# Memory attention and a bilinear feed-forward on one core: heads of batches 2 to 7 grouped by row half, three transposes for the means of k and v, and a new work list

## The chip, the cores and the metric

The kernel runs on one core of a Trainium2 chip. The metric is device time in microseconds (us) from the start of an execution to its end; the time given is the median of three executions. Beside it stands one execution that the hardware profiler recorded.

The engines are named as the profile names them: PE (matrix products), PEld (its weight loads), DVE (vector), ACT (scalar, activation functions), POOL (GpSimd) and SP (which issues transfers here). Each takes its instructions in the order in which the program lists them.

## The reference

For 8 batches, 8 heads, 576 tokens, head dimension 64 and 32 memory slots, all in float32:

```python
a = exp(phi - max(phi)); a = a / (sum(a, slots) + 1e-9)
k_m = einsum('bhsm,bhsd->bhmd', a, k)      # 32 weighted sums of k per head
v_m = einsum('bhsm,bhsd->bhmd', a, v)
scores = (q @ k_m.T) / sqrt(64)
attn = softmax(scores, slots)
x = (attn @ v_m), heads joined: 4608 tokens x 512
out = ((x @ w_a) * (x @ w_b)) @ w_out      # 512 -> 1536 -> 512
```

## The kernel before

**Per batch.** A batch has its heads on chip as 4 columns hp with two heads each: r = 0 on rows 0 to 63, r = 1 on rows 64 to 127. The eight heads are split into two groups g of four (j = 0 to 3). Inside a group every head has 32 rows (its memory slots) of the 128. Which head stands at (g, j) is told by `head(g, j)`; before, it crosses the two row halves: the heads of one group lie alternately on rows 0 to 63 and 64 to 127.

1. `exp_phi` (list name `exp`): exp of phi on ACT.
2. Means of k and v. In batches 2 to 7, `kv_sums` (`kv`, L286): 72 products on 64x32 tiles of PE into two banks `pkv`, one for each group; `take_kv` (`km`, L313, L318) divides on DVE and writes `rep`, six blocks of 128 columns: the even and odd columns of the k means for each group, each repeated four times, and the v means for each group, repeated twice; `kv_transpose` (`kvt`, L326, L327) turns the six blocks on PE with the identity into a bank `pT` and copies them to `kvT` on DVE. In batches 0 and 1, whose inputs come in halves, `sums` and `transpose` (`ks`, `vs`, `kt`, `vt`, L340 to L361) do the same in smaller parts.
3. `q_transpose` (`qt`, L269) turns q on DVE; `scores` (`sc`, `s`, L375) multiplies it with kvT on 32x32 tiles; `exp_scores` (`e`) takes exp on ACT. The division by the sum over slots has two forms: `denominators` and `normalise` (`den`, `nr`), or in batches 4 to 7 `ed`, `sm`, `tn`, `ad`. The result is the tile `A` of the batch.
4. `fold` (`v`, `hv`, L447) multiplies the means of v straight into w_a and w_b on 64x32 tiles, into banks `pva`; `take_fold` (`x`, `hx`, L460) copies them to `vab` on ACT and DVE.

**Feed-forward.** `up_half` (`a` and `b` with batch, block of 128 inner columns, half of the tokens; L621): two full products of 288 columns for each of `pa` and `pb`; ACT copies `pa` (L625), DVE multiplies with `pb` into `ht` (L628). The down projection works on pairs of blocks of 128 tokens in a seven-product scheme (`two_downs`, `d`, L550), 42 products of 256 columns for a pair. It takes sums of `ht` (`sum_tokens`, L534), which run on DVE where the list says `g` and on POOL where it says `h`, and sums of w_out (`T`, `V`).

**Order.** Nothing reorders the work: the string `PLAN` is walked from left to right (L632), and each word issues its instructions to the queues of their engines. A word such as `3kvt` is unit `kvt` of batch 3, `a2.5.1` is `up_half`, `d4` takes four products of the down projection, `F5` issues five idle products of 512 columns and `f5` five of 128 columns on a tile of zeros (`fill`, L211). Words such as `p1`, `k1`, `q1.0`, `v1`, `w256:512`, `o1` issue loads on POOL; `M` is a memset on POOL (L639).

Accumulators live in eight PSUM banks that are handed out in turn; tiles in `mid` have two buffers.

Of the kernel before, what the change touches and what calls it, by code (L numbers as in the profile page):

```python
# [25 lines left out]
f3 F1 O 0exp0 f1 f1 F2 p1 f2 f6 F7 w0:256 f2 f1 k1 f1 F3 0exp1 F5 f2 0qt0 q1.0 0ks0 0ks1 F5 0kt0 0qt1 M F2 0s0  # L26
w256:512 0qt2 0kt1 0e0 0den00 0qt3 0s1 0e1 F4 0den01 1exp0 0vs0 q1.1 0vt0 v1 0vs1 1exp1 F6 0nr00 0den10 0vt1
0den11 0hv0a 0hx0a 0nr10 0hv0b 0hx0b 0nr11 a0.1.0 b0.1.0 a0.0.0 F4 0nr01 1ks0 1ks1 b0.0.0 0hv1a 0hx1a 1kt0 1kt1
1qt0 1qt1 a0.0.1 a0.2.1 F1 b0.0.1 1s0 a0.1.1 0hv1b 1qt2 1qt3 0hx1b 1s1 1e0 1e1 b0.2.1 1den0 a0.2.0 b0.1.1 b0.2.0
1den1 1vs1 1vs0 1vt1 1nr0 1vt0 1nr1 a0.3.1 a0.3.0 1hv1b 1hx1b 1hv0b 1hv0a 1hx0a w512:1024 1hx0b b0.3.1 b0.3.0  # L30
1hv1a 0v1a 1hx1a 0x1a a1.0.0 a1.1.1 a1.1.0 a1.0.1 b1.0.0 b1.1.1 b1.1.0 a1.3.0 b1.0.1 a1.3.1 b1.3.0 b1.3.1 a0.5.0
0v1b 1v1a w1024:1536 0x1b 1x1a a1.2.0 1v1b 0v2a 1x1b o1 0x2a a0.7.1 b0.5.0 b1.2.0 b0.7.1 a0.7.0 b0.7.0 o5 a1.5.0
a1.2.1 b1.2.1 b1.5.0 a0.4.0 a0.6.0 b0.4.0 a0.4.1 a1.4.0 b0.6.0 b1.4.0 a0.9.1 0v2b 1v2b 1v2a 0x2b 1x2b a1.5.1
b0.4.1 1x2a b0.9.1 a0.8.0 a1.4.1 b1.5.1 o2 a0.5.1 a0.6.1 b0.8.0 a0.9.0 b0.6.1 b0.9.0 b1.4.1 a1.7.1 b0.5.1 b1.7.1
a0.8.1 b0.8.1 o0 a1.7.0 a0.10.0 b1.7.0 b0.10.0 a0.11.0 a1.9.0 o3 o4 b0.11.0 g0.0 b1.9.0 a1.6.1 k2 a1.6.0 p2 h0.3
a0.11.1 b1.6.1 b0.11.1 a1.8.1 a0.10.1 b1.6.0 v2 b1.8.1 g0.1 T01 a1.8.0 T00 V20 q2 T21 d1 2exp0 a1.9.1 d3 b0.10.1
p3 a1.10.0 d2 V10 g0.2 V11 d1 b1.9.1 2exp1 d1 a1.11.1 k3 d1 q3 T31 T30 d1 b1.10.0 b1.8.0 d1 b1.11.1 d4 h1.0 d2
2kv d4 2km d3 a1.11.0 d10 a1.10.1 2qt0 3exp0 d1 2kvt d2 h1.1 d1 2qt1 d12 2qt2 d3 2qt3 b1.10.1 g1.2 b1.11.0 v3 d1
2sc 2e0 d1 g1.3 d3 g2.0 d3 2e1 d1 2den0 h2.1 d8 p4 d8 2nr0 2den1 g2.2 2v0 2x0a 2x0b d2 2nr1 d10 2v1 d5 2x1a 3qt0
d3 g2.3 d3 2x1b d1 a2.3.0 a2.2.0 b2.3.0 b2.2.0 q4 k4 v4 a2.5.0 3exp1 b2.5.0 d2 3qt1 d4 a2.0.0 b2.0.0 d3 h3.0  # L40
a2.1.0 a2.4.0 2v2 3kv 3qt3 2x2a 3qt2 b2.1.0 2x2b d2 a2.11.1 a2.6.0 d4 3km a2.8.0 d1 q5 b2.4.0 d3 b2.6.0 d2 4exp0
d5 b2.11.1 d5 h3.1 d2 b2.8.0 a2.11.0 3kvt d2 a2.8.1 a2.7.1 b2.8.1 d2 a2.9.0 b2.7.1 3sc 3e1 3e0 g3.3 d1 b2.11.0
4qt0 a2.7.0 d2 a2.5.1 b2.5.1 b2.7.0 h3.2 3den0 d1 3nr0 4qt3 d1 b2.9.0 d2 a2.0.1 4qt2 a2.10.0 b2.0.1 p5 a2.4.1
b2.10.0 d1 k5 a2.10.1 d3 b2.10.1 d3 h4.0 4exp1 d1 a2.2.1 b2.4.1 3den1 d4 3v1 3x1a 4kv 3v0b 3x1b d3 3x0b d1 3nr1
d6 4km0 h4.1 a2.6.1 b2.2.1 a2.9.1 4qt1 a2.1.1 3v0a 3v2 d1 3x0a d2 3x2a d2 b2.6.1 3x2b d4 a3.9.0 d4 a3.5.0 d2
4km1 h4.2 b2.9.1 d1 a2.3.1 4kvt d1 b2.1.1 d1 b2.3.1 d2 5qt0 4sc a3.11.0 d1 h4.3 b3.5.0 5qt2 d5 4e1 d1 4e0 d1 v5
d6 b3.9.0 a3.0.0 g5.0 d1 h5.1 d3 4ed b3.11.0 d1 a3.3.0 d2 a3.10.1 b3.0.0 h5.2 5exp0 4sm0 q6 a3.1.0 d1 b3.3.0 d4
a3.3.1 d2 p6 d2 b3.10.1 a3.8.1 h5.3 d1 b3.3.1 b3.1.0 a3.6.0 b3.6.0 a3.7.0 a3.10.0 b3.8.1 d1 a3.1.1 b3.7.0 5qt1
d2 a3.8.0 a3.2.0 b3.10.0 d3 5exp1 a3.4.0 d1 b3.8.0 b3.1.1 d2 b3.2.0 k6 b3.4.0 4v0a 5kv 4x0a d1 a3.2.1 5km0
a3.4.1 5km1 d3 h6.0 h6.1 b3.2.1 d1 a3.9.1 d3 a3.5.1 d1 b3.4.1 b3.9.1 d5 4v0b 4x0b 4tn0 4v1 d1 h6.3 d3 4x1a d1  # L50
4x1b d2 a3.11.1 5kvt d1 p7 4sm1 a3.7.1 h6.2 d1 v6 d3 a3.6.1 d2 b3.5.1 b3.11.1 d1 5qt3 4v2 d4 4tn1 a3.0.1 d7 4x2a
4ad 6exp0 d1 b3.0.1 d6 4x2b b3.7.1 a4.11.0 b3.6.1 d1 a4.9.0 6exp1 d1 6qt0 b4.11.0 a4.7.0 a4.4.0 d4 b4.9.0 k7 d1
5sc 5e1 d1 5e0 d1 a4.0.0 d1 b4.4.0 d1 b4.0.0 a4.2.0 b4.2.0 d1 b4.7.0 d3 6qt1 d2 a4.4.1 d2 q7 a4.1.1 b4.4.1 5v0
5x0a 5x0b 6kv 5v1 h7.0 5x1a d3 6km0 a4.10.1 d1 5ed 6km1 d2 h7.3 h7.1 b4.1.1 h7.2 g8.0 d1 5x1b d2 h8.1 d1 a4.6.1
d4 b4.6.1 d4 a4.8.0 a4.5.0 5sm0 d1 v7 d1 h8.2 b4.10.1 a4.8.1 b4.8.0 a4.3.1 b4.5.0 d2 6qt3 d7 5v2 d2 5x2a d2
a4.1.0 d2 b4.3.1 7qt0 a4.3.0 d1 5x2b d1 b4.8.1 d1 7qt2 d1 b4.3.0 a4.5.1 d2 a4.10.0 b4.1.0 d2 6kvt 7exp0 d2 5tn0
d3 5sm1 a4.0.1 b4.5.1 d1 6qt2 d2 b4.0.1 d1 a4.6.0 d3 a4.7.1 d5 h8.3 d1 b4.10.0 d1 7exp1 d2 5tn1 d1 7qt1 a4.11.1
d3 6sc d5 6e1 d5 a4.2.1 d1 b4.7.1 d1 b4.6.0 5ad d1 a4.9.1 d1 h9.0 d1 b4.2.1 d3 6e0 b4.11.1 d1 b4.9.1 d1 a5.2.0
d1 a5.2.1 6ed g9.1 d1 b5.2.0 6v0a 6x0a 6v0b 7kv 6x0b b5.2.1 a5.11.0 b5.11.0 a5.8.0 a5.9.0 b5.8.0 h9.2 d1 7km0 d1
a5.3.0 d1 h9.3 d2 b5.9.0 b5.3.0 d2 a5.6.0 d1 g10.0 d1 h10.1 b5.6.0 a5.3.1 h10.3 d4 b5.3.1 d2 a5.1.0 d5 7qt3 d4  # L60
a5.7.0 d1 7km1 a5.7.1 b5.7.1 d9 b5.7.0 a5.5.0 d3 b5.1.0 d4 6sm0 b5.5.0 d3 a5.0.0 a5.1.1 d1 a5.10.0 d1 b5.0.0
7kvt d3 a5.0.1 d2 h10.2 b5.1.1 b5.0.1 d6 b5.10.0 a5.11.1 a5.10.1 6sm1 a5.4.0 d2 6v1 b5.10.1 6x1a d3 b5.4.0 d2
6x1b d1 b5.11.1 d1 a5.5.1 a5.9.1 6v2 6x2b b5.5.1 d1 6tn1 d1 a5.8.1 d1 6tn0 a5.6.1 d1 6x2a a5.4.1 d1 6ad b5.9.1
d4 7sc d1 7e1 7e0 b5.6.1 d2 b5.4.1 b5.8.1 a6.7.0 d1 7ed a6.9.0 7v0a 7v1 g11.0 d2 7x1a d2 g11.1 d2 a6.10.0 h11.3
h11.2 d1 h12.0 d3 7x0a 7sm0 a6.0.0 d2 b6.7.0 d2 b6.10.0 d4 b6.9.0 d5 a6.3.0 d7 a6.11.0 b6.11.0 b6.0.0 d1 a6.2.0
d5 b6.2.0 d1 a6.8.0 d1 b6.3.0 d1 7x1b d1 a6.5.0 h12.1 a6.10.1 b6.5.0 d4 7sm1 d4 h12.2 d3 a6.6.1 d2 g12.3 d3
b6.8.0 d6 a6.4.1 d3 b6.4.1 a6.9.1 d2 7tn1 b6.10.1 d1 7tn0 d3 7ad d2 b6.6.1 a6.2.1 a6.3.1 d1 a6.1.0 d1 b6.3.1
b6.2.1 d2 b6.9.1 d5 a6.8.1 a6.4.0 b6.1.0 b6.8.1 a6.11.1 b6.4.0 a6.6.0 b6.6.0 h13.0 a6.1.1 h13.1 a6.5.1 b6.11.1
d1 b6.5.1 d1 7v0b 7v2 d1 7x0b 7x2a a6.0.1 b6.1.1 d1 7x2b b6.0.1 d1 g13.2 d1 a6.7.1 d2 a7.11.0 d5 a7.6.0 a7.7.0
d7 g13.3 d1 b6.7.1 b7.6.0 b7.11.0 a7.0.0 d1 b7.7.0 d2 a7.2.0 d1 b7.0.0 d10 a7.1.0 a7.4.1 a7.3.0 d1 b7.2.0 b7.3.0  # L70
b7.1.0 d1 a7.10.1 a7.4.0 h14.0 h14.3 d7 b7.4.1 d2 a7.5.0 a7.10.0 g14.1 b7.5.0 d1 b7.4.0 b7.10.1 a7.5.1 a7.3.1
b7.5.1 d1 b7.10.0 a7.8.0 d1 a7.9.1 b7.3.1 d1 h14.2 a7.1.1 d1 b7.8.0 b7.9.1 a7.8.1 a7.9.0 d2 b7.9.0 d3 h15.0 d1
h15.1 d2 a7.2.1 b7.1.1 d3 a7.7.1 d15 b7.8.1 d3 g15.2 d4 a7.0.1 g15.3 d11 b7.0.1 d3 b7.2.1 d1 a7.11.1 d3 b7.7.1
d1 a7.6.1 d2 b7.11.1 d10 b7.6.1 g16.0 d6 g16.1 d5 g16.2 d1 g17.0 d11 h16.3 d8 h17.1 d24 h17.3 d13 g17.2 d28
# [4 lines left out]
def kernel(  # L79
# [171 lines left out]

    def units(b):

        u = {}
# [51 lines left out]
        def take_kv(gs=range(2)):  # L306

            if gs[0] == 0:
                t["rep"] = mid.tile([P, 6, P], F16, name="rep")
                t["rphi"] = small.tile([P, 2], F32, name="rphi")  # L310
            for g in gs:
                pkv, bank = t["pkv"][g]
                nc.vector.reciprocal(out=t["rphi"][:, g:g + 1], in_=pkv[:, 2 * D:2 * D + 1])  # L313
                km = pkv[:, 0:D].rearrange("p (d e) -> p e d", e=2).unsqueeze(2).to_broadcast([P, 2, 4, 32])
                vm = pkv[:, D:2 * D].unsqueeze(1).to_broadcast([P, 2, D])
                for out, x in ((t["rep"][:, 2 * g:2 * g + 2].rearrange("p e (z d) -> p e z d", z=4), km),
                               (t["rep"][:, 4 + g].rearrange("p (z d) -> p z d", z=2), vm)):
                    nc.vector.tensor_scalar(out=out, in0=x, scalar1=t["rphi"][:, g:g + 1], scalar2=None, op0=ALU.mult)  # L318
                banks.free(bank)

        def kv_transpose():

            t["kvT"] = mid.tile([P, 6, P], F16, name="kvT")
            pT = banks.tile([P, 6, P], F16, name="pT")
            for x in range(6):
                nc.tensor.transpose(out=pT[:, x, :], in_=t["rep"][:, x], identity=ident)  # L326
            nc.vector.tensor_copy(out=t["kvT"], in_=pT)  # L327
# [358 lines left out]
```

## Time and profile before

| what | value |
|---|---|
| median of 3 executions | 237.14 us (237.03 to 237.19) |
| profiled execution, own time | 237.06 us |
| its span on the core | 235.4 us |
| instructions | 7727 |
| PE busy | 226.6 us, 96% |
| PEld / DVE / ACT / POOL busy | 171.4 / 186.9 / 152.6 / 132.0 us |
| read from and written to HBM | 42.47 and 9.44 MB |

The page gives busy time for each engine, then the span in slices, the transfers, the chain that ended last, and groups of equal instructions with their mean duration and the idle time of their engine ahead of them. The duration of a matrix product there is longer than the time for which it holds PE, since products overlap; how long one holds PE is read from the distance between the starts of neighbours in the timeline.

### The profile page before, as it was taken

How to read it: one execution, taken by the hardware profiler on the slowest of the kernel's cores; microseconds unless marked ns; L12 is line 12 of the kernel's file. 1: busy time of each engine (PE TensorE's matmuls, PEld its weight loads, DVE VectorE, ACT ScalarE, POOL GpSimd, SP SyncE). 2: the span in 40 equal slices, each digit the busy share in tenths (PEclk: the TensorE clock that was granted, in tenths of full speed). 3: DMA queues.
4: the chain of work that ended last, by engine and by line, in shares of the span. 5: the costliest groups of instructions: out<-in, count | busy, mean ns of one | idle time of the engine just before them, and what ended most of it. 6: DMA issues, size and time to landing. Idle time of an engine off the chain costs nothing.

```text
span 235.4 us, 7727 instructions
## 1 busy us (share of the span) xinstructions
PE 226.6 (96%) x3075; PEld 171.4 (73%) x3075; DVE 186.9 (79%) x454; ACT 152.6 (65%) x398; POOL 132.0 (56%) x117
## 2 busy tenths in 40 slices
PE   7988899999999999999999999999999999999993
...
PEclk9999999999999999999999999999999999999999
...
GB/s 232 235 252 203 207 207 207 205 259 258 214 249 214 198 170 238 66 176 214 117 227 206 133 138 54 92 1 92 1 76 16 92 45 49 1 93 43 57 148 111
DMA packets 25748, 34.12 MB, mean 145 GB/s; under 512 B 2000, under 2 KB 19792, under 8 KB 25712
## 3 DMA queue, kind: packets, MB, share of 16 engines
...
q10 hardware_dynamic: 512, 0.79, 1.0%
...
q14 instruction: 12, 0.10, 0.1%
HBM read 42.47 MB, written 9.44 MB: 221 GB/s over the span
## 4 chain that ended last, share of the span: by engine, by line
PE 86%; DMA 7%; POOL 3%; DVE 1%; issue 0%
PE py L550 21%; PE pb L621 20%; PE pa L621 20%; PE pv L550 10%; PE pva L447 5%; PE px L550 5%; DMA q_sb<-in_q_dram 5%; DMA ht<-in_k_dram 2%; PE pkv L286 2%; PE pscore L375 1%; POOL kv_sb L639 1%; PE pT L326 1%; PE pD L398 1%; POOL wa_sb L159 1%; DVE kv_sb L217 1%; POOL wb_sb L160 1%
## 5 line engine op out<-in xcount | busy, mean ns | idle before, releaser
L625 ACT CAST a_sb<-pa 128x288 f16<-128x288 f32 x192 | 72.3, 407 | 38.1 <-PE pa L621 30.6
L628 DVE TENSOR_TENSOR ht<-a_sb,pb 128x288 f16<-128x288 f16 x192 | 80.1, 447 | 19.6 <-PE pb L621 12.0
L621 PEld LDWEIGHTS <-vab 128*128 128x128 f16 x768 | 73.8, 98 | 19.1 <-issue 3.0
L621 PE MATMUL pb<-A,vab 128*128 128x288 f16 x384 | 71.9, 286 | 0.0
L621 PE MATMUL pa<-A,vab 128*128 128x288 f16 x384 | 71.3, 286 | 0.6 <-DVE A L409 0.4
L534 POOL TENSOR_TENSOR h_sums<-ht 128x768 f16<-128x768 f16 x22 | 36.0, 1640 | 36.5 <-DVE ht L628 36.4
L550 PEld LDWEIGHTS <-h_sums 128*128 128x128 f16 x432 | 41.8, 98 | 9.0 <-issue 1.5
L550 PEld LDWEIGHTS <-ht 128*128 128x128 f16 x324 | 31.0, 98 | 8.5 <-issue 3.5
L460 ACT CAST vab<-pva 128x512 f16<-128x512 f32 (+1 forms) x60 | 31.3, 570 | 7.2 <-PE pva L447 6.8
L550 PE MATMUL py<-w_sums,h_sums 128*128 128x256 f16 x216 | 35.4, 273 | 0.0
L534 POOL TENSOR_TENSOR h_sums<-h_sums,ht 128x768 f16<-128x768 f16 x13 | 21.3, 1639 | 15.1 <-DVE h_sums L534 7.1
L460 DVE CAST vab<-pva 128x512 f16<-128x512 f32 (+1 forms) x44 | 26.8, 635 | 2.9 <-PE pva L447 2.8
L534 POOL TENSOR_TENSOR h_sums<-ht,h_sums 128x768 f16<-128x768 f16 x11 | 18.1, 1643 | 11.0 <-PE pa L621 5.9
L550 PE MATMUL pv<-w_sums,h_sums 128*128 128x256 f16 x108 | 19.3, 273 | 0.0
L557 ACT ACTIVATE u<-py 128x256 f32<-128x256 f32 x36 | 14.0, 390 | 8.1 <-PE py L550 6.2
L550 PE MATMUL px<-wo_sb,ht 128*128 128x256 f16 x108 | 19.0, 273 | 0.0
L550 PE MATMUL py<-wo_sb,ht 128*128 128x256 f16 x108 | 18.9, 273 | 0.0
L550 PE MATMUL py<-w_sums,ht 128*128 128x256 f16 x108 | 18.5, 273 | 0.0
L550 PE MATMUL pv<-wo_sb,h_sums 128*128 128x256 f16 x108 | 18.5, 273 | 0.0
L269 DVE STREAM_TRANSPOSE qT<-q_sb 128x288 f32<-128x288 f32 x32 | 14.5, 465 | 2.1 <-DMA q_sb<-in_q_dram 2.1
L260 ACT ACTIVATE exp_sb<-phi_sb 128x576 f16<-128x576 f32 x16 | 10.8, 687 | 6.0 <-DMA phi_sb<-in_phi_dram 6.0
L211 PE MATMUL pw<-warm 128*128 128x512 f16 (+1 forms) x59 | 13.2, 382 | 1.3 <-DVE warm L180 1.3
...
## 6 DMA issues: line engine op xcount, KB each, us to landing
...
wa_sb<-in_moe_w_a_dram POOLq DMA_DIRECT2D x2, 512.0 KB, 15.3
```

The source lines that it names most:

```text
L211: nc.tensor.matmul(pw[:, :cols], warm[:, :P], warm[:, :cols], start=True, stop=True)
L260: nc.scalar.activation(out=t["exp"][:, 2 * z:2 * z + 2, :, :], in_=phis[b][:, 2 * z:2 * z + 2, :].rearrange("p c (i m) -> p c i m", m=M), ...
L269: nc.vector.transpose(out=t["qT"][:, hp, :].bitcast(F32), in_=qs[b][:, hp, :].bitcast(F32))
L286: nc.tensor.matmul(t["pkv"][g][0][32 * j:32 * j + 32, 0:n], t["exp"][64 * r:64 * r + 64, hp, i, :], kvs[b][64 * r:64 * r + 64, 0:3 - given ...
L447: nc.tensor.matmul(t["pva", lo, z][g][0][32 * j:32 * j + 32, 0:hi - lo], t["kvT"][64 * r:64 * r + 64, 4 + g, M * j:M * j + M], w_sbs[z][64 ...
L460: engine_copy(out=vabs[b][z][:, g, lo:hi], in_=pva[:, 0:hi - lo])
L534: engine.tensor_tensor(out=out, in0=in0, in1=in1, op=op)
L550: nc.tensor.matmul(po, lhs[:, i], rhs[:, i], start=first and i == 0, stop=i == KH - 1, skip_group_check=not first)
L557: nc.scalar.mul(out=x, in_=po, mul=scale)
L621: nc.tensor.matmul(ps, vabs[b][x][:, g, P * i:P * (i + 1)], attn[b][:, g, HALF * hf:HALF * (hf + 1)], start=(g == 0), stop=(g == 1))
L625: nc.scalar.copy(out=a_sbs[b, i, hf], in_=ps)
L628: nc.vector.tensor_tensor(out=ht[:, i, t0:t0 + HALF], in0=a_sbs.pop((b, i, hf)), in1=ps, op=ALU.mult)
```

## The change

Batches 0 and 1 keep the crossed order of heads. From batch 2 on, group g holds the four heads with r = g, so that a group lies on one half of the rows. The transposed means of one group are then needed on that half of the rows alone, and both groups fit side by side in one block of 128 columns: `rep` and `kvT` have three blocks instead of six, and `kv_transpose` turns three. The two `kvT` of batches 0 and 1, which keep six blocks, get tiles of their own.

```diff
-    def head(g, j):
+    def crossed(g, j):
         jj = j ^ g
         return jj % 2, 2 * g + jj // 2
+    def straight(g, j):
+        return g, j
     def units(b):
+        side = b < 2
+        head = crossed if side else straight
...
-                t["rep"] = mid.tile([P, 6, P], F16, name="rep")
+                t["rep"] = mid.tile([P, 3, P], F16, name="rep")
...
-                km = ....unsqueeze(2).to_broadcast([P, 2, 4, 32])
-                vm = pkv[:, D:2 * D].unsqueeze(1).to_broadcast([P, 2, D])
-                for out, x in ((t["rep"][:, 2 * g:2 * g + 2].rearrange("p e (z d) -> p e z d", z=4), km),
-                               (t["rep"][:, 4 + g].rearrange("p (z d) -> p z d", z=2), vm)):
+                km = ....unsqueeze(2).to_broadcast([P, 2, 2, 32])
+                half = slice(D * g, D * (g + 1))
+                for out, x in ((t["rep"][:, 0:2, half].rearrange("p e (z d) -> p e z d", z=2), km),
+                               (t["rep"][:, 2, half], pkv[:, D:2 * D])):
...
-            t["kvT"] = mid.tile([P, 6, P], F16, name="kvT")
-            pT = banks.tile([P, 6, P], F16, name="pT")
-            for x in range(6):
+            t["kvT"] = mid.tile([P, 3, P], F16, name="kvT")
+            pT = banks.tile([P, 3, P], F16, name="pT")
+            for x in range(3):
...
-                t["kvT"] = mid.tile([P, 6, P], F16, name="kvT")
+                t["kvT"] = consts.tile([P, 6, P], F16, name=f"kvT{b}")
...
-                                t["kvT"][row:row + 32, 2 * g + dh, M * j:M * j + M],
+                                t["kvT"][row:row + 32, (2 * g if side else 0) + dh, M * j:M * j + M],
...
-                            t["kvT"][64 * r:64 * r + 64, 4 + g, M * j:M * j + M],
+                            t["kvT"][64 * r:64 * r + 64, 4 + g if side else 2, M * j:M * j + M],
```

The list is written anew from end to end. It has the same work units in another order, with these differences in number: 31 sums of `ht` on DVE (`g`) instead of 26, 41 on POOL (`h`) instead of 46, and 39 `F` and 18 `f` products instead of 40 and 19. The part between the first copies of folded weights and the fold of batch 0 into inner columns 512 to 1023, before:

```
... 0hv0a 0hx0a 0nr10 0hv0b 0hx0b 0nr11 a0.1.0 b0.1.0 a0.0.0 F4 0nr01 1ks0 1ks1 b0.0.0 0hv1a 0hx1a 1kt0 1kt1
1qt0 1qt1 a0.0.1 a0.2.1 F1 b0.0.1 1s0 a0.1.1 0hv1b 1qt2 1qt3 0hx1b 1s1 1e0 1e1 b0.2.1 1den0 a0.2.0 b0.1.1 b0.2.0
1den1 1vs1 1vs0 1vt1 1nr0 1vt0 1nr1 a0.3.1 a0.3.0 1hv1b 1hx1b 1hv0b 1hv0a 1hx0a w512:1024 1hx0b b0.3.1 b0.3.0
1hv1a 0v1a ...
```

and after:

```
... F1 F3 0hv0a M q1.1 0hx0a 0nr01 F2 0nr11 a0.0.1 a0.1.1 F1 a0.1.0 0hv0b F1 0hx0b v1 1ks0 1qt0 1ks1
w512:1024 b0.1.1 a0.0.0 1kt0 0hv1a 0hx1a b0.0.1 1qt1 b0.0.0 w1024:1536 b0.1.0 a0.3.0 0hv1b 1s0 1kt1 0hx1b 1e0
a0.2.0 1qt2 1den0 1qt3 a0.2.1 1s1 b0.2.0 1e1 1nr0 b0.2.1 1den1 a0.3.1 1vs1 1vs0 b0.3.0 1vt0 1vt1 1nr1 b0.3.1
1hv1b 1hv0b 1hv0a 1hx0a 1hx1b 1hx0b 0v1a 1hv1a ...
```

The memset `M` stood ahead of the loads `w256:512` and now stands behind them.

More of the change, by code (lines that the diff above doesn't have):

```diff
@@ L25 @@
 PLAN = """
[L26 to L74, printed above, removed]
+F9 f1 f1 F2 O f1 p1 f4 w0:256 f1 0exp0 f1 0exp1 f1 f3 F1 f1 F6 F1 k1 f4 0ks0 0qt0 q1.0 0ks1 0kt0 F2 0qt2 F2 0qt3
@@ new lines @@
+0qt1 0s0 F4 0e0 0kt1 0den00 F1 0s1 F3 0nr00 w256:512 0e1 1exp0 0den10 0vs1 0vs0 1exp1 0den01 0vt0 0nr10 0vt1
+0den11 F1 F3 0hv0a M q1.1 0hx0a 0nr01 F2 0nr11 a0.0.1 a0.1.1 F1 a0.1.0 0hv0b F1 0hx0b v1 1ks0 1qt0 1ks1
+w512:1024 b0.1.1 a0.0.0 1kt0 0hv1a 0hx1a b0.0.1 1qt1 b0.0.0 w1024:1536 b0.1.0 a0.3.0 0hv1b 1s0 1kt1 0hx1b 1e0
+a0.2.0 1qt2 1den0 1qt3 a0.2.1 1s1 b0.2.0 1e1 1nr0 b0.2.1 1den1 a0.3.1 1vs1 1vs0 b0.3.0 1vt0 1vt1 1nr1 b0.3.1
+1hv0b 1hv1b 1hv0a 1hx0a 1hx1b 1hx0b 0v1a 1hv1a 1hx1a a1.0.1 0x1a a1.1.0 b1.0.1 a1.0.0 b1.0.0 b1.1.0 a1.1.1
@@ new lines @@
+a1.3.0 b1.3.0 a1.3.1 a0.5.0 b1.1.1 b1.3.1 0v1b 0x1b a0.7.1 1v1a 1x1a 1v1b 1x1b 0v2a 0x2a a0.7.0 b0.5.0 b0.7.1
+a1.2.0 a1.5.0 b0.7.0 b1.2.0 a0.4.0 a1.2.1 b1.5.0 o1 a1.4.0 o2 b1.2.1 a0.9.1 b0.4.0 0v2b 0x2b 1v2b o0 1v2a 1x2b
+a0.5.1 a0.4.1 b1.4.0 b0.9.1 b0.4.1 a1.7.1 b0.5.1 o5 a1.4.1 a0.6.0 a1.5.1 b1.7.1 a0.8.0 b1.5.1 b1.4.1 b0.6.0
+a0.6.1 a0.9.0 b0.8.0 b0.9.0 a0.10.0 a0.8.1 b0.6.1 o3 1x2a o4 a1.7.0 p2 b1.7.0 a0.11.0 b0.11.0 b0.10.0 d1 b0.8.1
+a1.9.0 a1.6.0 g0.0 a0.10.1 a0.11.1 k2 b1.9.0 a1.8.1 h0.3 v2 b1.6.0 d1 b0.10.1 b0.11.1 T00 T01 a1.6.1 d1 b1.6.1
@@ new lines @@
+b1.8.1 q2 a1.11.1 d4 V20 g0.1 a1.10.0 T21 a1.8.0 V10 a1.9.1 2exp0 p3 d1 g0.2 V11 d1 k3 b1.9.1 d1 2exp1 q3 b1.8.0
+d1 T31 T30 b1.11.1 d2 h1.0 a1.10.1 d2 b1.10.0 d2 2kv 2km d6 a1.11.0 d8 2kvt d1 v3 d1 2qt0 2qt2 d6 2qt1 d1 2qt3
+d3 g1.1 d2 b1.10.1 d2 g1.2 d7 2sc 2e0 b1.11.0 g1.3 d6 2den0 d4 g2.0 2e1 d2 h2.1 d4 p4 d1 2v0 d1 2nr0 d2 g2.2
+2den1 d1 2x0a d1 2nr1 d16 2x0b d2 3qt0 d1 2v1 d2 2x1a h2.3 d4 a2.1.0 d2 2x1b a2.2.0 b2.2.0 a2.0.0 a2.5.0 d1
+3exp0 d5 b2.0.0 d1 b2.1.0 b2.5.0 d3 2v2 3exp1 3kv 2x2a 2x2b q4 a2.6.0 h3.0 d1 a2.4.0 a2.10.0 h3.1 3km 3qt2 d1 p5
@@ new lines @@
+k4 v4 3qt1 d7 a2.3.0 d1 h3.3 d1 b2.6.0 d1 b2.4.0 d2 3kvt d1 b2.3.0 d1 k5 d2 b2.10.0 3qt3 d1 a2.7.0 d2 4exp0
+a2.11.1 d2 a2.8.0 d3 b2.7.0 d1 b2.11.1 3sc 3e1 d1 a2.11.0 a2.9.0 h3.2 d1 3e0 d1 b2.11.0 b2.9.0 4exp1 d1 b2.8.0
+g4.0 a2.8.1 d2 b2.8.1 d2 a2.3.1 d1 a2.0.1 d1 5exp0 d1 a2.10.1 d1 4qt0 d2 p6 3den0 h4.3 q5 a2.4.1 b2.0.1 3nr0
+h4.1 b2.10.1 3den1 d2 v5 b2.3.1 a2.7.1 d3 a2.5.1 b2.4.1 4qt1 d1 5exp1 h4.2 a2.9.1 d3 b2.7.1 a2.2.1 4qt2 a2.1.1
+d3 b2.2.1 d2 3v1 3x1b 3v0b 4kv 3x0b 4km0 d2 4km1 d9 3x1a d1 b2.9.1 d1 b2.5.1 d2 3nr1 d8 4qt3 4kvt d2 3v2 3v0a
@@ new lines @@
+3x2a 3x0a d3 a2.6.1 d1 a3.5.0 3x2b d3 b2.1.1 a3.10.0 d2 a3.1.1 b3.10.0 b2.6.1 d4 a3.11.0 d1 g5.0 b3.11.0 4sc d1
+4e0 b3.5.0 4e1 d1 4ed d1 5qt0 d2 a3.8.1 h5.1 a3.7.0 b3.1.1 d2 a3.1.0 b3.8.1 d1 4sm0 d3 k6 b3.7.0 a3.0.0 a3.3.1
+h5.3 d1 a3.9.0 d3 h5.2 b3.0.0 d3 b3.1.0 d2 a3.6.0 b3.9.0 a3.3.0 b3.3.1 b3.6.0 a3.8.0 a3.9.1 b3.3.0 5qt3 a3.10.1
+b3.8.0 4tn0 d1 a3.2.0 q6 a3.4.0 b3.2.0 p7 b3.10.1 b3.4.0 b3.9.1 5kv 4v0a a3.11.1 5km0 4x0a d1 a3.0.1 d1 5km1
+h6.0 d5 5qt1 d5 4v1 4x1a 4v0b d2 4x1b d2 4sm1 d2 4x0b b3.0.1 a3.5.1 d6 a3.2.1 d3 6exp0 d3 4tn1 d1 b3.11.1 b3.5.1
@@ new lines @@
+d1 4v2 d1 4ad 4x2a d1 a3.7.1 b3.7.1 d1 h6.1 d2 a4.0.0 h6.3 4x2b d2 b3.2.1 g6.2 a4.2.0 b4.0.0 a3.4.1 5qt2 d2
+b4.2.0 d1 b3.4.1 7exp0 d4 a4.9.0 5kvt 6exp1 d2 v6 a4.11.0 q7 a3.6.1 b3.6.1 a4.7.0 b4.9.0 d3 b4.7.0 7exp1 b4.11.0
+5sc 5e0 5e1 6qt0 d1 a4.8.0 d1 h7.0 d1 5ed b4.8.0 d5 a4.1.0 d6 a4.1.1 d1 h8.0 5v0 h7.1 5x0a 5x0b 6kv 6km0 5v1
+5x1b d2 b4.1.0 6qt2 d1 k7 d3 b4.1.1 a4.3.1 d3 6km1 d2 a4.4.0 d1 5sm0 d1 a4.10.0 d1 a4.4.1 b4.4.0 v7 h7.2 b4.3.1
+d5 b4.4.1 d1 5x1a d4 h7.3 b4.10.0 d1 a4.7.1 d1 6kvt a4.5.0 d4 5v2 d2 5x2a d1 h8.1 a4.10.1 d1 h8.2 d1 5sm1 d3
@@ new lines @@
+a4.6.1 b4.7.1 5x2b a4.11.1 d2 b4.6.1 d4 6qt1 b4.5.0 d1 b4.10.1 5tn1 d2 a4.3.0 d1 6qt3 a4.9.1 a4.8.1 b4.11.1 h8.3
+7qt0 d2 a4.0.1 d2 5tn0 b4.8.1 b4.3.0 d2 b4.0.1 d3 7qt2 d4 b4.9.1 d2 6sc d2 6e0 d1 a4.6.0 5ad b4.6.0 g9.0 d3 h9.1
+a4.2.1 d4 a5.9.0 d1 7qt1 6e1 a4.5.1 b4.2.1 d1 a5.8.0 b5.9.0 b4.5.1 a5.2.0 d4 h9.3 d1 b5.8.0 d2 a5.11.0 d1 6v0a
+6x0a 6v0b 7kv d3 a5.3.0 d1 a5.7.1 7qt3 7km0 7km1 d2 b5.2.0 d5 a5.0.1 g10.0 6ed d1 b5.3.0 b5.11.0 h9.2 d4 b5.7.1
+6x0b d6 a5.0.0 h10.1 d1 a5.10.0 d1 a5.2.1 b5.0.1 b5.10.0 b5.0.0 a5.5.0 b5.5.0 b5.2.1 d2 a5.3.1 a5.6.0 d1 6v1
@@ new lines @@
+6x1b d1 6sm0 d1 a5.10.1 d4 b5.3.1 d1 a5.7.0 b5.10.1 b5.7.0 d1 6x1a d4 b5.6.0 6sm1 d2 6tn0 a5.5.1 d1 6v2 d1
+a5.4.1 d1 b5.5.1 d1 6x2a d9 a5.4.0 b5.4.1 d2 h10.3 a5.1.0 d1 6x2b b5.1.0 d2 a5.1.1 d1 h10.2 d1 6tn1 b5.4.0 d2
+7kvt g11.0 a5.8.1 b5.8.1 a5.6.1 d9 h11.1 d2 a5.9.1 d3 6ad 7sc b5.1.1 d3 b5.6.1 7e1 d2 h11.2 d3 a6.10.0 a6.11.0
+b6.10.0 a6.3.0 b5.9.1 a6.8.0 d5 a5.11.1 b6.3.0 g11.3 b6.11.0 b6.8.0 d1 7e0 7ed d1 b5.11.1 d8 a6.7.0 d5 7sm0 d3
+a6.9.0 b6.7.0 d1 a6.5.0 d1 b6.5.0 d1 a6.0.0 d4 h12.0 b6.0.0 g12.1 d1 a6.9.1 d3 7v1 7v0a 7x1b d4 7x1a d1 h12.2 d2
@@ new lines @@
+b6.9.0 d1 b6.9.1 d4 a6.4.0 7sm1 g12.3 a6.3.1 a6.10.1 d1 b6.3.1 d4 b6.4.0 b6.10.1 d2 a6.8.1 d1 b6.8.1 d2 7x0a
+a6.6.0 a6.2.0 a6.6.1 b6.6.1 d6 a6.7.1 d1 b6.2.0 d1 7tn1 7tn0 b6.6.0 a6.1.0 d1 a6.0.1 d1 b6.1.0 d4 b6.7.1 a6.11.1
+d3 b6.0.1 d1 a6.4.1 d1 b6.4.1 d2 h13.0 a6.1.1 a6.2.1 d1 b6.11.1 b6.1.1 d6 a6.5.1 d1 7v0b h13.1 7v2 d3 7ad 7x2a
+a7.6.0 d4 7x0b d2 a7.3.0 b6.5.1 d2 g13.3 d1 h13.2 b6.2.1 d5 h14.0 d4 a7.1.0 d3 a7.7.0 d2 b7.6.0 d5 7x2b b7.3.0
+d1 b7.1.0 d4 b7.7.0 d4 a7.0.0 a7.8.0 d3 a7.11.0 d3 b7.0.0 a7.4.1 d1 a7.3.1 b7.8.0 b7.4.1 d1 g14.1 a7.9.0 b7.11.0
```

6 lines of the change are left out of this document (5 added, 1 removed).

## The prediction

> **What bounds the kernel now.** First the page: busy times, slices and granted clock.
>
> ```profile
> span 235.4 us, 7727 instructions
> PE 226.6 (96%) x3075; PEld 171.4 (73%) x3075; DVE 186.9 (79%) x454; ACT 152.6 (65%) x398; POOL 132.0 (56%) x117
> PE   7988899999999999999999999999999999999993
> PEclk9999999999999999999999999999999999999999
> ```
>
> PE has nines from the sixth slice on, at the full clock. A busy PE can still be a PE that waits, so next the windows view cut at 33 us, where the fold of inner columns 512 to 1023 begins.
>
> ```profile
> 0.00:33.00 33.00, 28.31 (x563) 14.78 (x564) 18.14 (x53) 16.50 (x42) 19.06 (x31) 1.00 1.14 224
> 33.00:60.00 27.00, 27.00 (x343) 20.38 (x343) 26.26 (x66) 20.75 (x57) 17.16 (x16) 1.00 1.21 229
> 60.00:130.00 70.00, 70.00 (x1106) 54.39 (x1104) 61.68 (x149) 54.09 (x141) 51.20 (x42) 1.00 0.94 191
> 130.00:200.00 70.00, 70.00 (x803) 55.28 (x802) 59.85 (x141) 47.84 (x126) 30.49 (x21) 1.00 0.29 65
> ```
>
> Columns: stretch and length, then busy time with count for PE, PEld, DVE, ACT and POOL. From 33 us on PE is never free, and in the timeline its products follow each other at fixed distances (0.1225 us for 288 columns, 0.109 us for 256). The waits view agrees:
>
> ```profile
> PE pva L447 <- DMA wa_sb<-in_moe_w_a_dram: 1.3, 1, 1.3
> PE pw L211 <- DVE warm L180: 1.3, 1, 1.3
> PE pD L398 <- ACT E L388: 0.6, 1, 0.6
> PE pT L358 <- DVE kvm L350: 0.4, 1, 0.4
> ```
>
> These are its longest waits; all lie before 33 us, and a window of that view after 33 us is empty. So there are two parts. After 33 us a microsecond of PE work saved is a microsecond saved, as long as the other engines keep up. Before 33 us loads and the order of the list decide (DMA share 1.14; 59 of PE's products there are idle ones).
>
> **The transposes: the gain.** The timeline around batch 7's `kvt`:
>
> ```profile
> 162.47 0.41 PE L621 MATMUL pb<-A,vab 128*128 128x288 f16 x2
> 162.71 0.50 PE L326 MATMUL pT<-ident,rep 128*128 128x128 f16 x6
> 163.04 0.38 PE L550 MATMUL pv<-w_sums,h_sums 128*128 128x256 f16 x2
> ```
>
> Six transposes begin at 162.71 and the next product at 163.04: 0.33 us, or 0.055 us each. The 219 ns that the groups give one transpose counts overlap and is not the price. The change drops 3 x 6 batches = 18: 18 x 0.055 = **-0.99 us**, all on PE in the stretch that has no free time.
>
> **DVE and POOL: nothing on the path.**
>
> ```profile
> L318 DVE TENSOR_SCALAR rep<-pkv,rphi 128x256 f16<-128x256 f32 x12 | 5.8, 484 | 0.4
> L318 DVE TENSOR_SCALAR rep<-pkv,rphi 128x128 f16<-128x128 f32 x12 | 4.1, 342 | 0.0
> L327 DVE COPY kvT<-pT 128x768 f16<-128x768 f16 x6 | 3.3, 555 | 0.7 <-PE pT L326 0.7
> L350 DVE TENSOR_SCALAR kvm<-pk,rphi 128x64 f16<-128x64 f32 x8 | 2.3, 284 | 2.4 <-PE pk L340 2.2
> L361 DVE COPY kvT<-pT 128x256 f16<-128x256 f16 x4 | 1.1, 287 | 1.3 <-PE pT L358 1.3
> ```
>
> Columns after the bar: busy us in all and mean ns. The k part shrinks from 256 to 128 elements, 484 to about 342 ns; the v part from 128 to 64, 342 to about 284 (the same operation at L350); the copy from 768 to 384, 555 to about 354, on the line between 287 at 256 and 555 at 768. Per batch 2 x 0.142 + 2 x 0.058 + 0.201 = 0.60 us, in six batches -3.6 us. Five sums of `ht` move from POOL (1.64 us each, -8.2) to DVE (0.57 us each, the mean over its 26 sums, +2.9). DVE thus loses 0.7 us net. I count all of it as zero, because PE's own work covers it: PE waits for neither engine after 33 us. If the cover went, in 33 to 60 us where DVE is busy 26.26 of 27, every microsecond of late DVE would show; but that stretch holds mainly batches 0 and 1, whose units are unchanged.
>
> **The order of rows within a group: zero, against a rule.** Before, neighbours in `kv` and `sc` mostly alternate between row halves; after, four in a row lie on one half. The Trainium skill ("TensorE: Matmul & The Clock Gate", Part 3, The mechanism) says that a weight load overlaps running products only when its row group differs. By the rule the new order exposes loads: same-half neighbours rise from about 2 to 6 in every eight for `kv` (9 eights a batch) and `sc` (4) and fall from 3 to 0 for folds (6), so 4 x 13 - 3 x 6 = 34 a batch, 204 in all; at the 0.09 us of such a load, +18 us. The trace denies it with the old folds, which already have three such neighbours in eight:
>
> ```profile
> 128.04 0.41 PE L447 MATMUL pva<-wa_sb,kvT 64*32 64x512 f16 x8
> 128.27 0.40 PE L447 MATMUL pva<-wb_sb,kvT 64*32 64x512 f16 x8
> 128.48 1.02 PE L286 MATMUL pkv<-kv_sb,exp_sb 64*32 64x192 f16 x72
> ```
>
> Eight fold products take 0.23 and 0.21 us. One product of 512 columns would take 0.218 at the rate of L621 (0.1225 / 288 x 512). There is no room for one exposed load of 0.09. The 72 `kv` products, over at 129.26, take 0.78, nine eights of 0.087. I take 0; as bounds -0.2 (the new folds alternate everywhere) and +0.4 (0.07 a batch). Switches between tile shapes on PE, counted along both lists, are 84 and 84: 0.
>
> A second rule would make a gain of it: "TensorEngine Tiling (Array Packing)", Gotcha 1, has different row tiles unable to use one PSUM bank at once. The crossed order writes each bank from both halves and the straight one does not. If the rule held, the old eights would run in two halves and the new ones save some 0.08 us each. At 0.087 us per eight they ran together: 0, not a gain.
>
> **The start: about +0.1 us.** Loads are issued in the same order but for `M`, whose 2.09 us on POOL now follow `w256:512`. POOL's issues come earlier, yet the engines that carry them are full (DMA share 1.19 to 1.34 from 10 to 30 us) and the bytes ahead are the same, so I let every load land when it landed: wa 256:512 at about 24.3, q1.1 at 27.07, v1 at 29.9. If `M` did hold a load up, up to -0.3. The idle products: one `F` and one `f` less, under 0.3 us, in time that waits for loads anyway: 0. Up to the fold at 24.3 the new list has one more `a`/`b` word and `1kt0` behind it: 0.245 + 0.2 = 0.45 us ahead. Against that stands DVE:
>
> ```profile
> 23.17 0.44 DVE L628 TENSOR_TENSOR ht<-a_sb,pb 128x288 f16<-128x288 f16 x1
> 24.73 0.42 DVE L460 CAST vab<-pva 128x256 f16<-128x256 f32 x1 [1.11 <-PE pva L447]
> 27.07 0.84 DVE L269 STREAM_TRANSPOSE qT<-q_sb 128x288 f32<-128x288 f32 x2 [0.43 <-DMA q_sb<-in_q_dram]
> ```
>
> Before, DVE is idle when q1.1 lands and ends `1qt3` at 27.91. After, `1qt0` waits on DVE for q1.0 (about 23.2), with the `kvm` of `1ks1`, the next product into `ht` and a kvT copy queued behind it; `1qt2` and `1qt3` stand behind two more products into `ht` (0.45 each) and `0hx1b` (0.42). From 22.4 us I sum 5.9 us of DVE work and 0.4 of waiting: 28.7, or 0.8 later. So `1s1` and the softmax of batch 1 come 0.8 later, while v1 still lands at 29.9 and holds the last 3 us in either list. Both folds `1hv1a` and `0v1a`, over at 33.44 before, come out between 33.2 and 33.9; with the nearer end +0.1.
>
> **The sum.** Profiled execution 237.06 (span 235.4, 1.66 around it): -0.99 + 0.1 + 0 = 236.17. The median of three lies 0.08 above the profiled one, so I give 236.2. A measurement here tells about 0.2%, 0.47 us, from no change: faster means under 236.67, slower over 237.61.
>
> **The rivals.**
>
> *Forecast (0.58).* 18 transposes less, start within 0.35 of the old one: 235.8 to 236.6.
>
> *The start gives more (0.13).* With `0nr01` and `0nr11` earlier, PE stays ahead of the loads: 0.45 us, and 0.3 from `M`: 235.4 to 235.8. Against it speaks DVE's 0.8.
>
> *The gain goes at the start (0.18).* The late `1s1` pushes the tail of batch 1 past v1 and costs 0.5 to 1.0: 236.7 to 237.5. For it speaks the sum of 5.9 us; against it that 0.55 of the 8.7 us up to 33 still have PE idle, which can take up lateness.
>
> *Slower (0.11): batch 1's softmax turns into PE's wait.* Right behind the folds the list has `a1.0.1`, which needs `A` of batch 1; nothing can pass it. From `1s1` at 28.75: scores 0.45, exp 0.83, `den` 0.3, two logs 0.85, exp 0.70, DVE 0.46, and latencies: 32.6, against a need at 33.4. That has 0.8 us of slack. To end slower PE must lose 1.5 us at the start, so `A` would have to come at 34.9, 2.3 us later than I reckon. Three words on DVE that slip each by a wait of 0.8 would do that; I price it at 2 us: 238.1. Here I also put the row rule in a small form.
>
> **How the numbers follow.** Faster 0.58 + 0.13 = 0.71, same 0.18, slower 0.11. The range leaves out the slower case and the edges: 235.4 to 237.5. The likeliest case's own range is 235.8 to 236.6.
>
> **What would show it.** Right: L326 with 18 transposes, three in about 0.17 us; `rep` with 128x128 and 128x64 forms at about 342 and 284 ns; the kvT copy at about 354; no PE wait after 33 us; `0v1a` over between 33.2 and 33.9. Wrong: PE waits for DVE or ACT after 33 us (the new list starves it); 72 `kv` products over 0.9 us (row order costs); `A` of batch 1 named ahead of L621 near 33 us (the slower rival); PE idle in 60 to 200 us.

## The result, and the profile after

| kernel | executions | median | range |
|---|---|---|---|
| before | 4 | 237.16 us | 237.03 to 237.49 |
| changed | 4 | 235.59 us | 235.42 to 235.71, and one of 242.85 |

The ratio of changed to before is 0.9927, with a 95% interval of 0.9906 to 0.9948. The execution of 242.85 us is left out of that ratio, but the median of four counts it (the median of the three short ones is 235.46), and it is the one in the first profile. Such long executions came back in several kernels with the new list; the experiments below follow what makes them. Where the changed kernel is compared with the one before, the profile of a second run of it is used, `after_again` (235.86 us). Lines of code move by 7: L326 is now L333; in the runs below they move by other small numbers.

The page and the windows view of that second profile:

```profile
span 234.2 us, 7674 instructions
PE 225.2 (96%) x3055; PEld 169.9 (73%) x3055; DVE 184.1 (79%) x459; ACT 152.5 (65%) x398; POOL 123.8 (53%) x112
33.00:60.00 27.00, 27.00 (x339) 20.46 (x340) 25.92 (x66) 21.20 (x57) 16.93 (x16) 1.00 1.21 229
60.00:130.00 70.00, 70.00 (x1101) 54.30 (x1100) 59.94 (x152) 55.04 (x143) 48.79 (x41) 1.00 0.93 188
130.00:200.00 70.00, 70.00 (x805) 55.74 (x804) 58.31 (x141) 47.19 (x124) 35.30 (x24) 1.00 0.33 68
```

PE is still never free from 33 to 200 us, so time saved on PE is time saved. The transposes of one batch in the timeline:

```profile
166.84 0.38 PE L557 MATMUL pv<-wo_sb,h_sums 128*128 128x256 f16 x2
167.06 0.33 PE L333 MATMUL pT<-ident,rep 128*128 128x128 f16 x3
167.23 0.41 PE L628 MATMUL pa<-A,vab 128*128 128x288 f16 x2
```

Three transposes begin at 167.06 and the next product at 167.23: 0.17 us, where six took 0.33. The smaller operations on DVE, by groups (busy us and mean ns behind the bar):

```profile
L325 DVE TENSOR_SCALAR rep<-pkv,rphi 128x128 f16<-128x128 f32 x12 | 4.2, 351 | 0.4
L325 DVE TENSOR_SCALAR rep<-pkv,rphi 128x64 f16<-128x64 f32 x12 | 3.3, 276 | 0.0
L334 DVE COPY kvT<-pT 128x384 f16<-128x384 f16 x6 | 2.1, 352 | 0.0
```

The forecasts were 342, 284 and 354 ns.

The first profile shows something else. All of POOL's work from 64 to 74 us, and the vector sum that DVE starts in that time:

```profile
64.27 1.64 POOL L541 TENSOR_TENSOR h_sums<-h_sums,ht 128x768 f16<-128x768 f16 x1 [3.15 <-PE pv L557]
65.86 0.79 POOL L139 DMA_DIRECT2D phi_sb<-in_phi_dram  x1
65.95 7.66 DVE L541 TENSOR_TENSOR h_sums<-ht,h_sums 128x768 f16<-128x768 f16 x1
66.67 2.51 POOL L416 TENSOR_TENSOR A<-E,R 128x576 f16<-128x576 f16 x2
69.14 1.62 POOL L541 TENSOR_TENSOR h_sums<-ht 128x768 f16<-128x768 f16 x1
70.72 0.80 POOL L151 DMA_DIRECT2D q_sb<-in_q_dram  x1
71.53 1.64 POOL L541 TENSOR_TENSOR h_sums<-ht 128x768 f16<-128x768 f16 x1
73.26 1.85 POOL L541 TENSOR_TENSOR h_sums<-h_sums,ht 128x768 f16<-128x768 f16 x1
```

The sum `g2.2` lies on DVE for 7.66 us instead of 0.56. POOL works from 64.27 to 73.18 with no gap over 0.02 us; its next sum begins 0.08 us later, and only there does `g2.2` come through (it ends at 73.60), while that sum of POOL's takes 1.85 us instead of 1.64. All later work of DVE stands behind it, and PE waits for a copy of folded weights:

```profile
PE pva L454 <- DVE vab L467: 5.7, 1, 5.7
60.00:130.00 70.00, 64.28 (x920) 49.24 (x918) 60.58 (x135) 49.44 (x128) 42.55 (x36) 0.95 0.85 175
```

The wait is not all that is lost. The third number from the end of the second line is the clock granted to PE, and in smaller windows it is 1.00 from 60 to 68 us, 0.50 from 74 to 76 and 0.66 from 76 to 78: PE works on at half the clock for some 3.1 us after the wait, which by estimate costs 1.5 us more. With the wait of 5.7 that is the 7.2 us by which the span of 241.1 exceeds that of a short execution, 233.9. In this long execution the lower clock thus follows the wait and does not cause it.

### The profile page after: what moved, and what is told of

Read it like the earlier page. It is cut to its first block, busy times and chain, and to the rows that moved or that the text cites. A ratio compares the mean times of both kernels' runs of the same rounds, so it can differ in the third digit from the quotient of the medians.

```text
span 241.1 us, 7674 instructions
## 1 busy us (share of the span) xinstructions
PE 226.9 (94%) x3055; PEld 170.4 (71%) x3055; DVE 191.2 (79%) x459; ACT 152.5 (63%) x398; POOL 124.2 (52%) x112
## 4 chain that ended last, share of the span: by engine, by line
PE 81%; DMA 12%; DVE 4%; POOL 1%; issue 0%
PE py L557 20%; PE pa L628 19%; PE pb L628 19%; PE pv L557 10%; DMA wa_sb<-in_moe_w_a_dram 10%; PE pva L454 5%; PE px L557 5%; DVE h_sums L541 3%; PE pkv L293 2%; DMA ht<-in_k_dram 2%; PE pscore L382 1%; DVE kv_sb L218 1%; PE pT L333 0%; PE pD L405 0%; POOL phi_sb L139 0%
## 5 line engine op out<-in xcount | busy, mean ns | idle before, releaser
L628 PE MATMUL pa<-A,vab 128*128 128x288 f16 x384 | 72.1, 287 | 0.7 <-DVE A L416 0.7
L541 POOL TENSOR_TENSOR h_sums<-ht 128x768 f16<-128x768 f16 x20 | 32.8, 1642 | 35.5 <-DVE ht L635 35.4
L557 PE MATMUL py<-w_sums,h_sums 128*128 128x256 f16 x216 | 38.1, 277 | 0.0
L541 POOL TENSOR_TENSOR h_sums<-h_sums,ht 128x768 f16<-128x768 f16 x11 | 18.3, 1661 | 21.6 <-PE pv L557 7.6
L557 PE MATMUL pv<-w_sums,h_sums 128*128 128x256 f16 x108 | 18.8, 274 | 0.0
L541 POOL TENSOR_TENSOR h_sums<-ht,h_sums 128x768 f16<-128x768 f16 x10 | 16.4, 1644 | 2.1 <-DVE h_sums L541 1.8
L454 PE MATMUL pva<-wa_sb,kvT 64*32 64x512 f16 (+1 forms) x208 | 11.2, 374 | 6.5 <-DVE vab L467 5.7
L454 PEld LDWEIGHTS <-kvT 64*32 64x32 f16 x416 | 5.2, 89 | 13.6 <-DVE vab L467 6.0
L395 ACT ACTIVATE E<-pscore 128x288 f16<-128x288 f32 x32 | 11.2, 415 | 5.5 <-PE pscore L382 5.4
```

The source lines that it names most:

```text
L395: nc.scalar.activation(out=Ev[:, g, :, z, :], in_=pss, func=AF.Exp, scale=1.0 / (8.0 * CS))
L454: nc.tensor.matmul(t["pva", lo, z][g][0][32 * j:32 * j + 32, 0:hi - lo], t["kvT"][64 * r:64 * r + 64, 4 + g if side else 2, M * j:M * j + ...
L541: engine.tensor_tensor(out=out, in0=in0, in1=in1, op=op)
L557: nc.tensor.matmul(po, lhs[:, i], rhs[:, i], start=first and i == 0, stop=i == KH - 1, skip_group_check=not first)
L628: nc.tensor.matmul(ps, vabs[b][x][:, g, P * i:P * (i + 1)], attn[b][:, g, HALF * hf:HALF * (hf + 1)], start=(g == 0), stop=(g == 1))
```

## The experiments

Times are those of all executions of a kernel; "short" leaves out those over 242 us, which are called long.

**The changed kernel again.** No edit.

> The changed kernel once more, for a profile without the one vector sum of 7.66 us that the first profile shows at 66 us. First theory: that sum was held off by POOL's sums around it, by chance of timing; here every vector sum of this form takes 0.55 to 1.2 us, the span is about 233.7 us and the time 235.5 us, with PE never free after 33 us. Rival: the new list makes this collision each time; then the sum is again above 5 us and the time above 240 us.

Six executions: 235.34, 235.62, 235.86, and 243.04, 243.20, 244.46. Ratio of the short ones 0.9933 (0.9911 to 0.9954). In the profile of the execution of 235.86 no vector sum takes over 0.56 us: `g2.2` starts at 66.53, 0.08 us after POOL began to issue the same load, and is through before POOL's next product. Both expectations hold in part: the long executions are not rare, 4 of 10 with the first four, but they are not there each time.

**The new code with the old list.**

```diff
-PLAN = (new list)
+PLAN = (list of before)
```

> The new order of heads and the three transposes, with the list of before word for word. First theory: the 18 transposes are worth 18 x 0.055 = 0.99 us wherever they stand, and the list the rest: 236.2 us, 0.95 under before. Rival (the list makes the gain): 237.1 us, no change. Rival (relief of DVE pays as well): under 235.8 us.

236.11 us, all six from 236.02 to 236.27; ratio 0.9954 (0.9940 to 0.9969). That is 1.00 under before (237.11 in that run) and within 0.1 us of the first theory. There are no long executions.

**The old code with the new list.**

```diff
-PLAN = (list of before)
+PLAN = (new list)
```

> The crossed heads and six transposes of before, with the new list word for word. First theory: the list is worth what is left, 1.57 - 0.99 = 0.6 us, most of it before 33 us: 236.6 us. Rival (the list fits the new code alone): 237.2 us or more, with PE waiting after 33 us. Rival (the list makes it all): 235.6 us.

Six executions from 236.82 to 237.56, six from 244.3 to 245.95; ratio of the short ones 0.9995 (0.9980 to 1.0011). The list is worth nothing to the old code: the 0.6 us that it brings to the new code are missing. Its profile has one wait after 33 us that neither kernel shows, in the middle of a group of products. The profile calls it `issue`, which means that it shows nothing for which PE waited:

```profile
PE py L551 <- issue: 0.5, 1, 0.5
```

There the next product starts 0.73 us after the one before instead of 0.11. And the long executions do not need the three transposes: the old code has them with the new list.

**Six transposes in the changed kernel.**

```diff
-            for x in range(3):
+            for x in (0, 1, 2, 0, 1, 2):
```

> The changed kernel, in which kv_transpose of batches 2 to 7 turns its three blocks twice over into the same bank: six products again, with DVE's work as small as in the changed kernel. First theory: PE's time after 33 us is bare, so 18 products cost 18 x 0.056 = 1.0 us: 236.5 us. Rival (the transposes stood in slack and the smaller work on DVE made the gain): 235.5 us.

Twelve executions from 236.17 to 237.27, median 236.94; ratio 0.9985 (0.9973 to 0.9996). They fall in two sets: five from 236.17 to 236.68, and seven from 236.90 to 237.27. Against 235.5 for the changed kernel the lower set costs 0.7 to 1.2, as expected. The profiled execution belongs to the upper one and has the wait again, at the same product of the program as in the old code with the new list:

```profile
115.62 0.60 PE L557 MATMUL py<-wo_sb,ht 128*128 128x256 f16 x4
116.61 0.38 PE L557 MATMUL py<-wo_sb,ht 128*128 128x256 f16 x2 [0.39 <-issue]
```

So the transposes cost PE their full time, and DVE's smaller work, which this kernel keeps, does not make up for it. None of the twelve is long, although the list is the new one word for word.

**Order on one row half, made extreme.** The new code with the old list, and the products of a fold four by four on one half:

```diff
-                for j in range(4):
-                    for g in range(2):
+                for g in range(2):
+                    for j in range(4):
```

> The new code with the old list, in which fold issues the four products of a group one behind the other (four on one row half, then four on the other) instead of alternating. First theory: neighbours on one half cost nothing: 236.1 us, as new_code_old_list. Rival (the rule that a weight load overlaps products of other row groups alone): six exposed loads of 0.09 us in each of 36 eights, up to +19 us, and an eight of products longer than 0.22 us.

236.03 us; ratio 0.9957 (0.9944 to 0.9970), as with alternating folds. In the timeline eights still take 0.22 us and the 72 `kv` products 0.77:

```profile
127.32 0.41 PE L451 MATMUL pva<-wa_sb,kvT 64*32 64x512 f16 x8
127.54 0.40 PE L451 MATMUL pva<-wb_sb,kvT 64*32 64x512 f16 x8
127.76 1.02 PE L290 MATMUL pkv<-kv_sb,exp_sb 64*32 64x192 f16 x72
128.53 0.46 PE L451 MATMUL pva<-wa_sb,kvT 64*32 64x512 f16 x8
```

Four neighbours on one half load and run as fast as alternating ones; the rule about row groups that the prediction weighs does not hold for these tiles.

**Where in the list the rest lies.** The new code with lists put together at the first folds of inner columns 512 to 1023.

```diff
-PLAN = (new list)
+PLAN = (new list to "0v1a 1hv1a") + (old list from there)     # new_start_old_rest
+PLAN = (old list to "1hv1a 0v1a") + (new list from there)     # old_start_new_rest
```

> The new code; the list is the new one up to the first two folds of 0v1a and 1hv1a and the old one behind them. First theory: the new start is worth 0.35 us (0v1a and 1hv1a over at 33.1 instead of 33.4 us), the rest of the list some 0.3: 236.11 - 0.35 = 235.8 us, and no execution above 237. Rival (the start is worth nothing, the rest all 0.6): 236.1 us.

> The new code; the list is the old one up to the first two folds of 0v1a and 1hv1a and the new one behind them (w1024:1536 stands at the joint). First theory: 236.11 - 0.3 = 235.8 us in the executions without the held-off sum. Rival (the start makes all of it): 236.1 us. Rival (the rest makes all of it): 235.5 us.

New start, old rest: 236.19 us over twelve executions from 235.99 to 237.74 (ratio 0.9961, 0.9944 to 0.9977), no gain over 236.11, though its profile, of an execution of 236.74, has a wait of the `issue` kind too. One execution is above 237, against the expectation. Old start, new rest: 235.70 us over five (0.9939, 0.9927 to 0.9951), 0.4 under. The rest of the list makes the gain, and the first theory, which split it evenly, is wrong.

**The held sum, taken off DVE.**

```diff
-... 2nr0 d2 g2.2 2den1 ...
+... 2nr0 d2 h2.2 2den1 ...
```

> The changed kernel with one word of its list changed: the vector sum g2.2, the one of 7.66 us, is done by POOL (h2.2). First theory: the executions of 243 to 246 us that only kernels with the new list showed come from that one sum, which starts on DVE just ahead of a row of POOL operations and is held off by them; with it on POOL (1.64 us there) every execution takes 235.3 to 236.0 us. Rival: the long executions come from elsewhere; then about 4 in 10 still take over 242 us.

Eleven executions from 236.74 to 237.0 and no long one, which fits the held sum of the first profile as the cause. It is not proof by itself, since `turns_twice`, where the sum stays on DVE, has no long one either. The time is 1.2 over the short executions of the changed kernel, which was not expected: POOL is late instead, and PE waits for the product that normalises batch 2.

```profile
PE pa L625 <- POOL A L413: 1.2, 1, 1.2
```

**The row of POOL operations, broken.** One load word moved, in the new code and in the old code, both with the new list:

```diff
-... d2 h2.1 d4 p4 d1 2v0 ...
+... d2 p4 h2.1 d4 d1 2v0 ...
```

> The changed kernel with one word of its list moved: the load p4, which POOL issues right behind the sum h2.1, stands ahead of h2.1. Then POOL's work behind h2.1 is no longer one unbroken row, since 2nr1's product has to wait for ACT. First theory (the 7.66 us of the vector sum g2.2 are the time in which POOL leaves no gap): no execution over 238 us, and 235.4 to 236.0 us in all. Rival (the long executions have nothing to do with this row): about 4 in 10 over 242 us.

> Old code with the new list, of whose 12 executions 6 took 244 to 246 us, and with the same word p4 moved ahead of h2.1. First theory: no execution over 239 us; about 237.0 us. Rival: half of them over 244 us.

New code: six executions from 235.53 to 236.02, median 235.80, ratio 0.9935 (0.9917 to 0.9952). Old code: twelve from 236.90 to 238.39, ratio 1.0005 (0.9991 to 1.0019). No long execution in 18, against 10 of 22 in the same two kernels with the word in its old place: as far as 18 executions tell, breaking the row removes them. But the row is not enough to bring them. In `turns_twice` POOL's row is whole and `g2.2` starts 0.09 us behind the load, and none of 12 is long; what spares that kernel is not shown. The kernel before has the same sum 0.08 us behind the same load (66.42 and 66.34), but there POOL rests 0.05 us between its two products, and behind them stand three loads where the new list has a sum, a load and a sum; none of its 67 executions is over 238.81 us. The timeline of the new code with the word moved:

```profile
66.18 1.27 POOL L413 TENSOR_TENSOR A<-E,R 128x576 f16<-128x576 f16 x1
66.25 1.62 DVE L538 TENSOR_TENSOR h_sums<-ht,h_sums 128x768 f16<-128x768 f16 x1
68.00 1.28 POOL L413 TENSOR_TENSOR A<-E,R 128x576 f16<-128x576 f16 x1 [0.55 <-ACT R L411]
```

Here `g2.2` starts behind POOL's first product, is held until that ends at 67.45, and comes through, over at 67.87, in the 0.55 us in which POOL waits for ACT.

**The joined list again.** No edit to `old_start_new_rest`.

> old_start_new_rest once more (new code, old list up to the first folds of inner columns 512 to 1023, new list behind them), as the candidate that is under both kernels: 235.7 us in every execution. Rival: with the new rest of the list some executions take over 242 us here too.

Five executions from 235.60 to 236.02 and one of 243.77: the rival is right, the hazard is in the rest of the list. Of the versions with the new code and the new rest, `phi_load_first` is the one to take: it is as fast as the short executions of the changed kernel (ratio 0.9935 against 0.9927 and 0.9933), and none of its six is long.

## Why the prediction was right or wrong

The forecast was 236.2 us and faster; measured were 235.59 and faster, 1.57 under before where 0.9 had been forecast. That lies in the stated range of 235.4 to 237.5, but below the 235.8 to 236.6 of the forecast case. And it lies there by luck: only one of the four executions was long. In `after_again` three of six were, and the median of the same kernel is 239.45 us, out of the range; no case of the prediction has this cause. By its steps:

- **The transposes, -0.99: right.** The new code alone gave -1.00. Worked out from the starts of PE's products, the time from the first product behind `0v1a`/`1hv1a` to the last start is 197.54 us before and 196.54 in the new code with the old list, and the groups of products between differ in the transposes alone: 2.01 and 1.00 us.
- **Row order, 0: right.** In the same two profiles `kv` products take 5.03 and 5.03 us, scores 2.56 and 2.56, folds 11.33 and 11.34; `folds_by_half` shows the same from the other side. The rule of "TensorE: Matmul & The Clock Gate" (Part 3, The mechanism) would have cost 18 us, and the bank rule of "TensorEngine Tiling (Array Packing)" (Gotcha 1) would have shortened the eights; neither happened.
- **The start, +0.1: small, as forecast; its sign is open, and one term was wrong.** The folds were over at 33.07 and 33.66 in the two profiles of the changed kernel, where 33.2 to 33.9 were forecast, against 33.44 before. Over all runs, eight profiles with the new start have 33.07 to 33.66 and five with the old one 33.30 to 33.73, so single executions scatter by more than the term. The wrong term is the 5.9 us of DVE work up to `1qt3`. In the changed kernel's first profile:

```profile
23.03 0.28 DVE L357 TENSOR_SCALAR kvm<-pk,rphi 128x64 f16<-128x64 f32 x1
23.23 0.47 DVE L276 STREAM_TRANSPOSE qT<-q_sb 128x288 f32<-128x288 f32 x1
23.62 0.13 DVE L356 RECIPROCAL rphi<-pk 128x1 f32<-128x1 f32 x1
27.10 0.83 DVE L276 STREAM_TRANSPOSE qT<-q_sb 128x288 f32<-128x288 f32 x2
```

  An operation of 0.47 us is followed 0.39 later: recorded durations on DVE overlap as those on PE do. The prediction took the distance between starts for PE and the duration for DVE. By distances the chain, from 22.83 on, takes 5.1 us and ends at 27.93, not 28.7, level with 27.91 before. In `after_again` it does end late, at 28.54, but not from its length: it begins 0.31 later and waits 0.28 for PE.
- **The list behind 33 us, 0: wrong by 0.43.** The same stretch takes 196.54 us with the old list and 196.11 with the new one (`after_again`; 196.13 and 196.12 in the two profiles of old start, new rest). 0.28 of that are three lost times between products of `up_half` and the down projection that only the old list has, at 152.55, 172.79 and 173.10 in the profile before (0.12, 0.08 and 0.09). The first of them lies in these four products, which hold PE for 0.60 us instead of 4 x 0.1225:

```profile
152.19 0.65 PE L621 MATMUL pa<-A,vab 128*128 128x288 f16 x4
152.79 0.40 PE L621 MATMUL pb<-A,vab 128*128 128x288 f16 x2
```

  The rest are tenths up and down at products beside other kinds: scores, folds and `den` take 0.12, 0.11 and 0.09 less, `kv` 0.08 more. The prediction counted switches of tile shape and found 84 and 84. The count is right, in the traces too, but equal numbers did not make equal prices; why, no run shows. With the transposes this term makes 1.43 of the 1.57 us; what is left is less than the start scatters. This term and not a better start brings the time to where the case "the start gives more" had it.
- **DVE and POOL, nothing on the path: right in the short executions, wrong in the long ones.** Their own times shrank as forecast. What was missed is that POOL's operations can hold off a DVE sum with two inputs. The profile before has such a sum, which the prediction's mean of 0.57 us over 26 sums hides:

```profile
225.40 1.64 POOL L534 TENSOR_TENSOR h_sums<-ht 128x768 f16<-128x768 f16 x1
226.29 1.17 DVE L534 TENSOR_TENSOR h_sums<-ht,h_sums 128x768 f16<-128x768 f16 x1
```

  It ends 0.42 us after POOL's operation, as `g2.2` does in the long profile (0.43) and in `phi_load_first` (0.42). The slower rival looked for a late softmax of batch 1; what PE waits for in the long profile is a copy of folded weights behind one held sum of batch 2, 5.7 us. Of the prediction's own signs of being wrong, PE waiting for DVE after 33 us and PE idle in 60 to 200 us came true there.

Left open: the waits of the `issue` kind (0.66 to 0.73 us between two starts), which appear in four of the profiles. In the three with the new list and six transposes they come at the same product, in `new_start_old_rest` at another; no run was made for them. Counted through PE's products the two places are 256 apart. PE's 6150 products and weight loads go with 24 packets of 16 KB on queue `q8 instruction`, so a packet holds, by estimate, 256 of them or 128 products, and the two places are just two packets apart. A packet of instructions that comes late is therefore a candidate; but profiles without the wait have the same packets, and no run tells the two apart. The wait also does not explain all of what the old code loses with the new list: without its 0.62 us the stretch there is 197.38, only 0.15 under before, and its folds take 11.47 us against 11.23 in `after_again`. Why the new list brings the old code nothing and the new code 0.5 to 0.6 us is thus shown in part only.
